# Block 0's q on GpSimd's DMA queue, in a fused attention and feed-forward kernel with a written-out order

## The chip, the cores and the metric

The kernel runs on one core of a Trainium2 chip. The metric is the time of one execution on the device in microseconds (us). A core has five engines with instruction queues of their own: TensorE (PE, matmuls; its weight loads are listed apart as PEld), VectorE (DVE), ScalarE (ACT), GpSimd (POOL) and SyncE (SP, which here only issues DMAs). Each works through its queue in order and waits on semaphores for the others. SP, ACT and POOL can issue DMAs.

## The reference

Chunked causal attention over 4 batches, 8 heads, 768 positions and 64 dimensions, and then a gated feed-forward layer on the 3072 tokens of 512 numbers. From each chunk of 32 keys a minimum and a maximum are formed, from these an upper bound for each query and chunk, and each query looks at the six chunks with the highest bounds:

```python
ub = sum(maximum(q * k_min, q * k_max), axis=-1)      # per query and chunk, causal
top_chunks = argsort(ub)[..., -6:]
scores = where(chosen & causal, q @ k.T / 8, -1e9)
x = softmax(scores) @ v                               # (3072, 512)
xn = x / sqrt(mean(x * x) + 1e-6) * rms_g
out = (silu(xn @ w_gate) * (xn @ w_val)) @ w_out      # d_ff 1536
```

## The kernel before, in words

The work is cut into 12 blocks of 256 tokens (batch b, third m of the sequence), taken in the order of ORDER (L340): the blocks with m = 0 of all four batches first. "Block 0" is (0, 0), "block 1" is (1, 0). Each block has two head groups of four heads (g = 0, 1; operation names end in it). For each block:

- **Loads.** load_qk (L431) brings k and q into the tiles kraw and qraw (128 partitions: four heads x 32 rows). For blocks 0 to 2 (PACKED) each of the two comes in four DMAs, one for each head of a group (a = 0 to 3), with 32 partitions and both head groups in each: 128 KB a DMA. load_v (L456) brings v in two halves, load_w (L464) and load_wo (L469) the feed-forward weights in three thirds each (wg0 to wg2, wv0 to wv2, wo0 to wo2), all of these cast to bf16 on the way and issued by POOL. "load q0020" is q of block (0, 0), head 2.
- **Selection.** DVE turns k and q (turn, L636), reduces k to minima and maxima (ext0, ext1, L651), dk subtracts (L657); bd0 and bd1 place them for PE (L676); PE forms the bounds (upper, L540); DVE turns them back (ubn), bars the future (bar), finds the sixth largest (top), compares (mk) and turns the mask (mt); swap copies it for the other half. half (L643) makes bf16 copies of k and q.
- **Attention.** PE forms the scores (L760, the mask by L771), ACT the exponentials (exp, L810), POOL cuts the triangle (tri, L780), PE multiplies with v (values, L836), DVE divides (rden L851, norm L855). Blocks 0 and 1 do this in two parts (a and b).
- **Feed-forward.** square (ACT, L872), rms (POOL), scale, the turn of x on PE (turn, L916), xsT; then the gate matmuls wg and wv (L960), tanh, tg, vcopy, hh, and project (L1007), out, store. For block 0 the gates go by halves of 128 tokens in pieces of four column tiles: "wg(0, (0,)).4" is block 0, first half, tiles 4 to 7, which need wg1; the pieces .0 need wg0 and wv0, the pieces .4 wg1 and wv1, the pieces .8 wg2 and wv2.

None of this is put in order at run time. The kernel records every operation with its engine (and for some a choice of engines), and the class Plan holds two lists, STEPS and SLOTS (L47, L156): the order in which the recorded operations are issued with the engine of each, and the buffer that each takes. STEPS was found by a search with a planner's costs. Negative numbers in it are fills: matmuls on the identity that keep PE going where the planner saw nothing for it (keep_busy, L1071; narrow ones of 128 columns, wide ones of 512).

Every DMA goes through dma (L370). Its queue is the engine's that issues it. For waiting on them the program has eight semaphores for the DMAs of SP and ACT together and others for POOL's, given out in turn: a DMA first waits for the landing of the one that had its semaphore before. In the program before, the first eight DMAs of SP and ACT are block 0's k (two by each) and q (ACT: heads 0 and 3; SP: heads 1 and 2); then come block 1's eight on SP (k heads 0 and 1, q 0 and 1, k 3, q 2 and 3, k 2). The first load of block 2 also waits for wg1, that of block 3 for wo0 (HELD). POOL issues, behind its first memsets, wv0, v of block 0 (first half), wg1, v of block 0 (second half), v of block 1 (first half), wg0, then relu and the first triangles, v of block 1 (second half), wv1; later wg2, wv2 and the thirds of wo.

Of the kernel before, what the change touches and what calls it, by code (L numbers as in the profile page):

```python
# [11 lines left out]
ACT = mybir.ActivationFunctionType  # L12
# [21 lines left out]
class Plan:  # L34
# [13 lines left out]
        123, 228, 233, 155, 3, 99, 249, 244, 27, 257, 276, 83, 34, 203, 139, 281, 67, 268, 107, 315,  # L48
        131, 75, 115, 291, 380, 396, 323, 412, 538, 428, 466, 299, 404, 473, 482, 420, 443, 490,
        436, 545, 42, 307, 388, 498, 522, 506, 515, 179, 594, 529, 611, -2624, -320, 616, 562, 601,  # L50
        672, 554, 626, 571, 681, 50, 578, 457, 786, 587, 634, -82, -82, 792, 642, 689, 650, 57, 848,
        699, 802, 810, 9, 818, 857, 658, 826, 865, 834, 1098, 665, 875, 841, -176, 704, 451, 1042,
        -112, 736, 912, 713, 1114, 1107, 721, 1058, 1185, -146, 880, 1049, 1066, 19, 731, 1660, 746,
        331, 922, 889, 1130, 1628, 897, 754, 1075, 1644, 930, 1684, -274, -114, 1248, 1170, 961,
        760, 1676, 1082, 1091, 907, 195, 936, 1257, 1362, 1668, -80, 1192, 1138, 971, 1177, 1636,
        1202, 1147, 977, 1210, 770, 1154, 1163, 778, 1123, 1265, 946, -112, 984, 1652, 954, 1368,
        1218, 1001, 994, 1275, 1424, 1226, 1433, -51, 1312, 1378, 8384, 1011, 1234, 1441, 1322,
        1242, 1386, 8344, 1330, 147, 1451, 1017, 1394, 1402, 339, 1280, 1410, 8369, 1418, 1024,
        1289, 347, 1488, 8336, 1498, 1297, 1034, 355, 8401, 1506, 1456, 8353, 1307, 8480, 8410,
        1537, 363, 8362, 1336, 8497, 8488, 1547, 1346, 1762, 1473, 8528, 8506, 1465, 1851, 8513,  # L60
        1354, 1483, 1778, 8536, 8545, 8379, 1553, 1706, 1512, 8561, 8392, 1522, 371, 1530, 1834,
        1560, 1577, 8523, 8432, 1570, 8417, 8554, 1587, 8696, 8449, 1722, 8571, 8688, 8458, 8721,
        1730, 1593, 8584, 8705, 1802, 1739, 171, 2001, 1747, 1600, 8714, 1755, 8576, 8609, 1610,
        1841, 8731, 1856, 8440, 1713, 2212, 1866, 8427, 1794, 2228, 8736, 8593, 1874, 2260, 1811,
        8465, 1771, 2268, 8602, 8784, 2276, 1882, 2244, 1890, 8792, 1818, 1827, 1898, 8475, 8801,
        1906, 8753, 8832, 8817, 1699, 8762, 1912, 2220, 8810, 8849, 8619, 2008, 2308, 1921, 8744,
        2236, 2018, 1691, 1937, 2026, 2252, 2034, 8624, 8769, 2042, 8858, 1931, 1785, 2050, 8779,
        2284, 2057, 2324, 8888, 2292, 2354, 3050, 2064, 2363, 2300, 8632, 1947, 2073, 2316, 2370,
        8656, 2347, 2332, 2378, 2089, 2868, 2426, 2083, 8913, 2804, 8641, 2387, 2820, 2450, 2099,
        1952, 2844, 2442, 8827, -51, 2104, 8664, 2828, 1962, 2410, 8880, 2852, 8673, 2459, 2114,  # L70
        2395, 2900, 1970, 2417, 2403, 1976, 2122, 2836, 8840, 8897, 2482, 2884, 1986, 8928, 8906,
        8865, 2466, 2475, 2499, 3611, 2507, 1994, 8923, 2128, 8945, 2512, 2924, 2138, 2146, 2153,
        2916, 8875, 2161, 2860, 8936, 2522, 3476, 8954, 2171, 8976, 2812, 2530, 2538, 8684, 2946,
        2177, 3508, 2546, 8961, 2186, 2908, 2554, 8971, 2892, 2962, 2561, 2192, 2876, 2986, 9008,
        2433, 3484, 2339, 2201, 3010, 3524, 3532, 2491, 3034, 3540, 3019, 2970, 2568, 3492, 3003,
        3066, 8984, 2577, 9136, 3083, 8994, 2593, 2587, 3026, 9040, 4148, 9153, 3516, 2603, 2656,
        3116, 9162, 9057, 2979, 3043, 9048, 4283, 2953, 3500, 9066, 2665, 9004, 3058, 9096, 3075,
        4212, 9073, 2675, 3108, 9088, 3618, 2681, 163, 9083, 4252, 9121, 3634, 9144, 3092, 9105,
        3642, 2691, 3100, 9240, 9114, 9169, 3588, 2608, 9131, 9016, 9265, 3556, 2618, 2626, 2696,
        4164, 9025, 2632, 2706, 2714, 2720, 9179, 4236, 9184, 2730, 2745, 3572, 2642, 2650, 4220,  # L80
        2738, 3131, 9232, 9201, 3682, 4228, 3123, 2753, 9192, 4180, 9210, 211, 9249, 4244, 3706,
        2763, 3136, 9217, 9258, 2777, 9227, 9280, 3146, 3596, 2769, 5596, 3625, 9275, 9288, 3154,
        3658, 3564, 2993, 3580, 3162, 2784, 3675, 9313, 3548, 9328, 3691, 2793, 4196, 3722, 2931,
        4260, 4172, 9297, 3170, 4204, 9400, 9306, 4268, 4860, 3178, 9496, 9323, 9425, 9036, 3738,
        3185, 4156, 9392, 3698, 3651, 4188, 3755, 9336, 4290, 9409, 3603, 3764, 3192, 4330, 9521,
        3780, 9488, 3747, 9418, 3201, 3772, 3715, 4402, 9435, 9345, 9440, 4306, 3217, 9360, 3730,
        4347, 4417, 3788, 4339, 9457, 4354, 4876, 9505, 3667, 9466, 8652, 3211, 3232, 4378, 4452,
        2939, 9514, 4884, 9536, 3241, 5532, 4314, 3227, 4444, 9448, 3803, 9553, 4428, 3249, 3795,
        9562, 9544, 4868, 4370, 9473, 3304, 1620, 9569, 4386, 4322, 3808, 4436, 4394, 3313, 9579,
        4916, 3329, 9592, 4908, 3818, 9483, 4892, 4297, 9368, 4924, 3826, 9617, 3834, 3344, 3323,  # L90
        4940, 9377, 4980, 3339, 3256, 3353, 4972, 3842, 3280, 4900, 9584, 4459, 3290, 3361, 4932,
        3266, 3850, 9531, 9632, 3274, 9601, 3298, 3857, 3368, 9610, 5548, 3392, 3378, 9649, 4956,
        9627, 9640, 3386, 3402, 4964, 3417, 3410, 3864, 5580, 9658, 4275, 3425, 5644, 9680, 5002,
        3873, 9356, 4363, 5106, 4948, 3889, 3435, 5564, 5066, 9665, 9388, 3458, 3904, 4465, 5628,
        3442, 9675, 5612, 9712, 3913, 5018, 3883, 3452, 5026, 3899, 3921, 5090, 3468, 5042, 3976,
        5082, 4472, 5059, 3985, 5604, 5122, 5035, 4411, 4001, 9688, 4482, 3995, 9720, 9697, 5139,
        4016, 4490, 4498, 5049, 4011, 5148, 3928, 9729, 6308, 3952, 4025, 3938, 6356, 5098, 9792,
        3962, 4506, 5172, 4033, 9840, 3970, 5156, 3946, 9809, 4514, 5164, 4040, 9865, 9800, 9818,
        5620, 4521, 6332, 4050, 5714, 9832, 5572, 5114, 5588, 4592, 9849, 5179, 5652, 4058, 4064,
        5636, 5187, 4601, 9826, 9928, 6316, 5011, 4074, 9858, 4089, 5540, 187, 5075, 9880, 4082,  # L100
        6244, 4609, 5723, 6340, 5192, 6364, 4097, 6292, 9953, 4528, 4107, 5202, 9897, 9920, 4537,
        9906, 6324, 4114, 9752, 9937, 5556, 4130, 4547, 4553, 4124, 9968, 5730, 9777, 9946, 4563,
        4568, 9985, 4140, 5786, 9875, 5129, 9976, 5674, 4577, 91, 6260, 9994, 9888, 5803, 4585,
        6426, 4995, 5812, 9744, 9914, 6284, 4616, 10002, 6276, 9761, 5738, 4640, 9740, 5820, 4626,
        9770, 4664, 6268, 6442, 10072, 4673, 5690, 6348, 6980, 4634, 10256, 4689, 4683, 5210, 7628,
        5218, 5747, 10089, 7020, 10080, 10281, 219, 9963, 4650, 4704, 10098, 4658, 4987, 10120,
        6300, 4713, 6252, 5226, 10208, 7036, 10105, 5754, 5795, 5828, 10137, 10160, 4721, 9787,
        10146, 10168, 6506, 5698, 4728, 6521, 5234, 10177, 5707, 6540, 10008, 5683, 10193, 5762,
        7644, 10115, 5241, 6386, 7028, 10186, 5836, 10225, 4737, 6402, 6548, 10248, 10203, 6450,
        7676, 10128, 4745, 10234, 6988, 6371, 9708, 6410, 10016, 5771, 6916, 10296, 6490, 4699,  # L110
        10025, 7636, 10265, 5248, 6532, 10154, 10313, 4776, 6556, 10274, 5257, 6466, 6996, 4752,
        5273, 5267, 6948, 6474, 10304, 5843, 6956, 4762, 4770, 10036, 5667, 5288, 10322, 4786,
        10216, 5778, 5851, 5297, 7755, 7652, 4794, 10040, 4801, 7660, 10330, 6419, 4809, 5283, 7004,
        10242, 7012, 5305, 6483, 6435, 6498, 4819, 5856, 6457, 10291, 5360, 5866, 7692, 10048, 7724,
        5369, 4826, 5312, 6932, 5336, 5385, 6940, 5379, 10336, 6964, 5346, 5322, 10057, 5874, 5395,
        5330, 7684, 6569, 5882, 5659, 4836, 5400, 6562, 4842, 6576, 5409, 5354, 4852, 5890, 10368,
        5417, 5898, 7732, 6586, 6513, 7098, 5906, 10344, 7115, 6924, 5424, 7708, 10354, 5448, 7740,
        5912, 5434, 5458, 10068, 7058, 10376, 7748, 5921, 5442, 7067, 10496, 6594, 10364, 6602,
# [987 lines left out]
```

## Time and profile before

| | |
|---|---|
| median of 3 runs | 294.74 us (293.15 to 296.25) |
| the profiled execution's own time | 293.79 us |
| its span in the profile | 292.1 us |
| PE busy | 279.0 us, 4718 matmuls |
| DVE, ACT, POOL busy | 215.7, 207.1, 167.8 us |
| DMA | 31.94 MB moved, mean 109 GB/s |
| granted TensorE clock | full in all 40 slices |

The span is shorter than the execution's time by what lies around it. "Busy" counts instructions that compute; a PE that is busy may be doing fills. A line of a group reads: source line, engine, operation, what it writes <- what it reads, count, then the busy time and the mean of one. In a timeline a row begins with its start and duration in us from the span's start, and ends with the number of instructions merged and, in brackets, how long the engine stood idle before it and what ended that. In the chain of waits a row is start, duration and what the chain went through. A row of the DMA issues has the size of one and the median time from issue to landing; for a single DMA that is its own. A row of waits has the total, the count and the longest. A row of windows has, for PE, PEld, DVE, ACT and POOL in turn, the busy time in that stretch and the number of instructions.

### The profile page before, as it was taken

The page shows a single profiled execution, that of the slowest core. Times are in us where ns is not written, and L with a number is a line of the kernel's source. Part 1 is how long each engine was busy: PE and PEld are TensorE (multiplying, and loading weights), DVE is VectorE, ACT ScalarE, POOL GpSimd, SP SyncE. Part 2 cuts the span into 40 slices and gives each one's busy share as a digit, 9 for nine tenths or more (in the row PEclk, how much of TensorE's full clock was granted, in tenths as well). Part 3 has the DMA queues.
Part 4 walks back from the last instruction along what each step waited for, and adds up shares of the span by engine and source line. Part 5 has one row for each costly group of instructions (what it writes and reads, how often), then busy time and mean ns, then how long its engine had stood idle before and what let it go on. Part 6 is the DMA issues. An engine that isn't in the chain of part 4 may idle for free.

```text
span 292.1 us, 11448 instructions
## 1 busy us (share of the span) xinstructions
PE 279.0 (96%) x4718; PEld 214.8 (74%) x4746; DVE 215.7 (74%) x626; ACT 207.1 (71%) x355; POOL 167.8 (57%) x268
## 2 busy tenths in 40 slices
PE   7979999999999899999999999999999999999994
PEld 7637887668877757888676786688678967688663
DVE  3778887889898799799989999987564715374240
ACT  2958887678888898877876595877679766564421
POOL 9649789879888785567683385427125116113410
PEclk9999999999999999999999999999999999999999
DMA  7999999988589584459599816912012300311022
GB/s 177 210 193 224 204 207 134 168 132 127 115 159 159 133 161 87 106 102 168 99 187 139 147 31 92 122 11 74 0 43 69 21 2 3 110 45 30 2 108 72
DMA packets 86388, 31.94 MB, mean 109 GB/s; under 512 B 74816, under 2 KB 81728, under 8 KB 86336
## 3 DMA queue, kind: packets, MB, share of 16 engines
q1 hardware_dynamic: 55776, 22.82, 33.9%
q0 software_dynamic: 29712, 7.87, 27.1%
q10 hardware_dynamic: 848, 0.53, 0.9%
q8 instruction: 37, 0.61, 0.9%
q14 instruction: 15, 0.12, 0.1%
HBM read 28.58 MB, written 6.29 MB: 119 GB/s over the span
## 4 chain that ended last, share of the span: by engine, by line
PE 84%; DMA 7%; DVE 5%; issue 2%; ACT 1%; DVEq 0%; SPq 0%
PE F L960 43%; PE F L1007 19%; PE S L760 7%; PE F L836 7%; DMA kraw<-in_k_dram 6%; PE S L771 3%; PE F L522 3%; DMA xsT<-xs 1%; PE F L540 1%; DVE kx L651 1%; DVE kT L636 1%; DVE xnat L855 1%; PE F L916 1%; DVE xs L890 1%; DVE tg L971 0%
## 5 line engine op out<-in xcount | busy, mean ns | idle before, releaser
L810 ACT ACTIVATE pt<-S 128x1024 bf16<-128x1024 f32 (+3 forms) x104 | 85.5, 858 | 29.7 <-PE S L771 26.4
L982 POOL TENSOR_TENSOR hh<-tg,vs 128x512 bf16<-128x512 bf16 x48 | 55.5, 1165 | 46.4 <-DVE tg L971 29.1
L960 PE MATMUL F<-xsT,wg 128*128 128x256 bf16 (+1 forms) x640 | 72.4, 262 | 0.2 <-DMA xsT<-xs 0.2
L960 PE MATMUL F<-xsT,wv 128*128 128x256 bf16 (+1 forms) x640 | 71.8, 262 | 0.6 <-issue 0.5
L1007 PE MATMUL F<-wo,hh 128*128 128x512 bf16 (+1 forms) x272 | 65.7, 370 | 2.3 <-issue 0.6
L971 DVE SCALAR_TENSOR_TENSOR tg<-th,F 128x512 bf16<-128x512 bf16 x72 | 48.3, 678 | 25.9 <-ACT th L967 19.6
L960 PEld LDWEIGHTS <-wg 128*128 128x128 bf16 x640 | 55.9, 98 | 9.2 <-issue 0.9
L960 PEld LDWEIGHTS <-wv 128*128 128x128 bf16 x640 | 56.2, 98 | 8.5 <-issue 1.0
L967 ACT ACTIVATE th<-F 128x512 bf16<-128x512 f32 x72 | 42.5, 599 | 13.9 <-PE F L960 12.6
L780 POOL TENSOR_SCALAR_AFFINE_SELECT pt<-pt 128x512 bf16<-128x512 bf16 x48 | 31.6, 665 | 27.9 <-ACT pt L810 27.7
L1007 PEld LDWEIGHTS <-hh 128*128 128x128 bf16 x300 | 27.5, 98 | 25.8 <-issue 1.0
L979 ACT ACTIVATE vs<-F 128x512 bf16<-128x512 f32 x48 | 28.5, 599 | 9.8 <-PE F L960 6.5
L760 PE MATMUL S<-qb,kb 32*128 32x256 bf16 (+1 forms) x800 | 32.8, 253 | 0.3
L651 DVE TENSOR_REDUCE kx<-kT 128x16 f32<-128x512 f32 x48 | 31.1, 669 | 0.2
L836 PE MATMUL F<-VX,pt 128*128 128x65 bf16 x672 | 27.5, 194 | 2.9 <-DMA VX<-in_v_dram 1.7
L836 PEld LDWEIGHTS <-pt 128*128 128x128 bf16 x672 | 25.4, 98 | 6.5 <-issue 3.3
L975 DVE TENSOR_TENSOR hh<-tg,F 128x512 bf16<-128x512 bf16 x24 | 16.1, 681 | 10.3 <-PE F L960 10.0
L760 PEld LDWEIGHTS <-kb 32*128 32x128 bf16 x800 | 13.6, 92 | 13.1 <-issue 11.6
L376 POOL DMA_DIRECT2D VX<-in_v_dram x24 | 22.7, 947 | 0.0
L771 PE MATMUL S<-mtd,chunkrow 32*128 32x128 bf16 (+2 forms) x384 | 20.3, 203 | 0.7 <-DVE xnat L855 0.7
L855 DVE TENSOR_TENSOR xnat<-F,rden 128x256 bf16<-128x256 f32 x48 | 19.5, 415 | 0.7
L771 PE MATMUL S<-mto,chunkrow 32*128 32x128 bf16 (+2 forms) x384 | 19.9, 203 | 0.0
(73 smaller groups left out, 337.3 us busy)
## 6 DMA issues: line engine op xcount, KB each, us to landing
out_dram<-osb SPq DMA_DIRECT2D x23, 256.0 KB, 3.0
kraw<-in_k_dram SPq DMA_DIRECT2D x72, 64.0 KB, 3.3
qraw<-in_q_dram SPq DMA_DIRECT2D x72, 64.0 KB, 3.1
VX<-in_v_dram POOLq DMA_DIRECT2D x24, 128.0 KB, 5.1
QX<-qT SPq DMA_DIRECT2D x32, 64.0 KB, 2.4
wv<-in_moe_w_val_dram POOLq DMA_DIRECT2D x3, 512.0 KB, 8.5
wg<-in_moe_w_gate_dram POOLq DMA_DIRECT2D x3, 512.0 KB, 13.5
wo<-in_moe_w_out_dram POOLq DMA_DIRECT2D x3, 512.0 KB, 10.2
```

The lines of the kernel that those rows point to most:

```text
L651: plan.op(f"ext{n}{J}", "DVE", 0.585, 0.67, lambda n=n, op=op: VE.tensor_reduce(out=at(kx)[:, g, n], in_=at(kT).rearrange("p h (j c x) -> ...
L760: TE.matmul(s[a // 2][:, a % 2, c0:c0 + q1 - q0], kbt[r, t, ks], qbt[r, t, q0:q1], start=(t == 0), stop=(t == 1 and not mask), skip_group_ ...
L771: TE.matmul(o, chunkrow[r, BLK * kg + P * e:BLK * kg + P * (e + 1)], mv, start=False, stop=(d == 1), skip_group_check=True)
L780: GE.affine_select(out=d, in_=d, compare_op=ALU.is_ge, fill=0.0, base=0, pattern=[[0, 4], [1, P]], channel_multiplier=-1)
L810: lambda pt=pt, hs=hs, c0=c0, c1=c1, x=sc[hp]: SE.activation(out=at(pt)[:, hs, c0:c1], in_=at(x)[:, :, c0:c1], func=ACT.Exp, scale=SCALE), ...
L836: TE.matmul(o[:, a, :], p_[:, a, off:off + P], vt[:, e, 4 * g + a, :], start=(kb_ == 0 and a == 0), stop=(kb_ == nkb - 1 and a == 3), skip ...
L960: TE.matmul(at(p_)[:, n * W:(n + 1) * W], w[:, g, ht * P:(ht + 1) * P], at(xT)[:, g, x0:x0 + W], start=(g == 0), stop=(g == NP - 1), skip_ ...
L967: plan.op(f"tanh{U}.{hp}", "ACT", 0.48, 0.6, lambda th=th, gp=gp: SE.activation(out=at(th), in_=at(gp), func=ACT.Tanh, scale=0.5), pri - 0 ...
L971: VE.scalar_tensor_tensor(out=at(tg), in0=at(th), scalar=1.0, in1=at(gp), op0=ALU.add, op1=ALU.mult), pri - 30, reads=[th, gp], writes=[tg ...
L979: plan.op(f"vcopy{U}.{hp}", "ACT", 0.48, 0.6, lambda vs=vs, vp=vp: SE.activation(out=at(vs), in_=at(vp), func=ACT.Copy), pri + 0.1, reads= ...
L982: plan.op(f"hh{U}.{hp}", "POOL", 1.11, 1.16, lambda tg=tg, vs=vs, hh=hh: GE.tensor_tensor(out=at(hh), in0=at(tg), in1=at(vs), op=ALU.mult) ...
L1007: TE.matmul(at(op)[:, cs], at(key)[:, o:o + P], wo[:, ht, cs], start=(ht == 0), stop=(ht == NHT - 1), skip_group_check=True)
```

## The change

load_qk gets two sets. A tensor in WHOLE is loaded in two DMAs, one for each head group g, each over all 128 partitions (256 KB), and not in four DMAs of 32 partitions; one in BYPOOL is issued by POOL. Both sets hold block 0's q alone. So four DMAs of SP and ACT become two of POOL. The recorded operations are fewer by two, and STEPS and SLOTS are new throughout.

```diff
+    WHOLE = {(0, 'q')}
+    BYPOOL = {(0, 'q')}
...
     def load_qk(i, nm, src):
         b, m = ORDER[i]
         key = (nm + "raw", b, m)
-        first = True
-        for a in (0, 2, 1, 3):
...
+        todo = []
+        if (i, nm) in WHOLE:
+            for g in range(NG):
+                sv = src[b].rearrange("(g a) (m r j) d -> g m a r (j d)", g=NG, m=NBLK, r=32)[g, m]
+                todo.append((f"g{g}", sv, lambda g=g: at(key)[:, g].rearrange("p j h d -> p (j h d)"), 8, 0.09, (g,)))
+        else:
+            for a in (0, 2, 1, 3):
...
+        first = True
+        engs = ("POOL",) if (i, nm) in BYPOOL else ("SP", "ACT") if i == 0 else ("SP",)
+        for x, sv, dst, packets, cost, gs in todo:
+            dma(f"load {nm}{b}{m}{x}", engs, sv, dst, packets, cost,
+                loads_due(i, nm == "q"), writes=[key + (g,) for g in gs],
...
```

In the new program the first eight DMAs of SP and ACT are block 0's k and then, on SP, block 1's q head 0 and k heads 0, 3 and 1; the other four of block 1 (q 2 and 1, k 2, q 3) follow, each behind the landing of one of block 0's k loads or of block 1's first q load. POOL issues, behind two memsets, the identity's steps and two more memsets, q of block 0 (group 0), a memset, q (group 1), v of block 0 (first half), wg1, v (second half), wv0, and after the first small steps of the selection v of block 1 (first half), wg0, its second half, wv1; later wg2, wv2 and the thirds of wo. dk of block 0's first group moves from DVE to POOL. The load of ACT's table moves from behind block 0's first exponentials to ACT's start.

DVE's order in the first blocks, where it differs most: pat stands before and own behind the first turns of k; block 1's k is turned (group 1) ahead of block 0's top of group 1, and (group 0) ahead of its mk and mt; then come one reduction of block 1, rden of block 0, the turn of block 1's q, rden, another reduction, and the two norms. Before, block 0's mt came first, then the turns of block 1's q and k, two reductions, the two rden, a third reduction and the two norms.

PE's order up to the first gate holds the same operations. Of fills there are 87 narrow and 24 wide (before 92 and 34); one of two wide ones now stands ahead of wg(0, (0,)).8, and the one between values of block 2 is gone. After the first gates, one values operation of block 1 and the turn of its first half come ahead of the first use of wv1, in which the two halves' .4 pieces now follow each other.

More of the change, by code (lines that the diff above doesn't have):

```diff
@@ L433, in load_qk @@
         key = (nm + "raw", b, m)
-        first = True
-        for a in (0, 2, 1, 3):
-            rows = slice(32 * a, 32 * (a + 1))
-            if i in PACKED:
-                sv = src[b].rearrange("(g a) (m r j) d -> a m r g (j d)", a=4, m=NBLK, r=32)[a, m]
-                todo = [(sv, lambda rows=rows: at(key)[rows].rearrange("r g j h d -> r g (j h d)"), 4, 0.12, (0, 1))]
-            else:
-                todo = []
+        todo = []
[5 more added lines that the diff above has]
+            for a in (0, 2, 1, 3):
+                rows = slice(32 * a, 32 * (a + 1))
+                if i in PACKED:
+                    sv = src[b].rearrange("(g a) (m r j) d -> a m r g (j d)", a=4, m=NBLK, r=32)[a, m]
+                    todo.append((f"{a}0", sv, lambda rows=rows: at(key)[rows].rearrange("r g j h d -> r g (j h d)"),
+                                 4, 0.12, (0, 1)))
+                    continue
@@ L442, in load_qk @@
                 for g in range(NG):
                     sv = src[b, 4 * g + a, BLK * m:BLK * (m + 1), :].rearrange("(j r) d -> r j d", r=32)
-                    todo.append((sv, lambda rows=rows, g=g: at(key)[rows, g].rearrange(
+                    todo.append((f"{a}{g}", sv, lambda rows=rows, g=g: at(key)[rows, g].rearrange(
                         "r j h d -> r j (h d)"), 16, 0.019, (g,)))
-            for k_, (sv, dst, packets, cost, gs) in enumerate(todo):
-                dma(f"load {nm}{b}{m}{a}{k_}", ("SP", "ACT") if i == 0 else ("SP",), sv, dst, packets, cost,
-                    loads_due(i, nm == "q"), writes=[key + (g,) for g in gs],
-                    takes=[(key, nm + "raw")] if first else (), reads=() if first else [key],
-                    behind=[HELD[i]] if i in HELD and first else ())
-                first = False
+        first = True
@@ L453, in loads_due @@
+        engs = ("POOL",) if (i, nm) in BYPOOL else ("SP", "ACT") if i == 0 else ("SP",)
+        for x, sv, dst, packets, cost, gs in todo:
+            dma(f"load {nm}{b}{m}{x}", engs, sv, dst, packets, cost,
+                loads_due(i, nm == "q"), writes=[key + (g,) for g in gs],
+                takes=[(key, nm + "raw")] if first else (), reads=() if first else [key],
+                behind=[HELD[i]] if i in HELD and first else ())
+            first = False
     def loads_due(i, n):
```

278 rows, old and new, of tables (SLOTS, STEPS) are left out of this document.

## The prediction

> **What bounds the kernel now.** I read the page first, then the chain of waits from 0 to 40 us, the waits of PE, the timeline of each engine over the first 40 us, and the landing times of single DMAs.
>
> ```profile
> span 292.1 us, 11448 instructions
> PE 279.0 (96%) x4718; PEld 214.8 (74%) x4746; DVE 215.7 (74%) x626; ACT 207.1 (71%) x355; POOL 167.8 (57%) x268
> DMA  7999999988589584459599816912012300311022
> ```
>
> PE is busy for 96% of the span, and the third row shows the transfers full from slice 2 to slice 8 (a slice is 7.3 us), that is until about 58 us. So the kernel is bound by PE's own work, except where PE has nothing real to do yet: at the start. There the chain that sets the end runs through a load of block 1's k, and from it through DVE, ACT and PE to the first feed-forward matmuls:
>
> ```profile
> 9.67 7.49 DMA kraw<-in_k_dram
> ...
> 25.43 1.79 PE F L960 x32
> ```
>
> That load is issued only at 9.67 because of the program's eight DMA semaphores for SP and ACT together: block 0's k and q take all eight, and each later load waits for the landing of the one eight places earlier; this one waits for block 1's first load. It lands at 17.16. DVE turns it, and only behind that stand, in DVE's order, block 0's rden and norm (to 21.09), then on the other engines square, rms, scale, the turn of x, and the first gate at 25.27. From there on PE runs almost without a break, as its waits and its timeline show:
>
> ```profile
> PE F L836 <- DMA VX<-in_v_dram: 1.7, 1, 1.7
> PE F L836 <- issue: 1.0, 1, 1.0
> PE S L771 <- DVE xnat L855: 0.7, 1, 0.7
> ```
> ```profile
> 25.27 1.05 PE L960 MATMUL F<-xsT,wg 128*128 128x128 bf16 x16
> ...
> 33.15 1.06 PE L960 MATMUL F<-xsT,wv 128*128 128x128 bf16 x16
> 34.05 0.42 PE L836 MATMUL F<-VX,pt 128*128 128x65 bf16 x8
> 34.31 1.05 PE L960 MATMUL F<-xsT,wv 128*128 128x128 bf16 x16
> 35.20 0.39 PE L916 MATMUL F<-ident,xs 128*128 128x128 bf16 x4
> 35.42 1.24 PE L960 MATMUL F<-xsT,wg 128*128 128x128 bf16 x16
> ```
>
> Only the wait of 1.7 us for v lies ahead of the first gate; the one of 0.7 lies between the first two rows of the timeline. So whatever brings the stream of gate matmuls forward by x us, and keeps it fed, shortens the span by x.
>
> **The change part by part.**
>
> *The loads of block 1.* Block 0's q leaves SP and ACT (four DMAs), so the eight semaphores hold block 0's k and four loads of block 1 at once. The last load of block 1's k then waits for one of block 0's k loads, the first DMAs of the program, and is issued near 4.5 (an estimate: block 0's k is whole at 5.09, when DVE turns it) instead of 9.67. With the 7.49 us of the chain's row it lands at 12.0, which I take, since all eight loads are in flight together. The ends are 9.6 (with the 5.1 us of the row for q below) and no gain at all, 17.16.
>
> *DVE's new order.* DVE now turns block 1's k before it finishes block 0's second head group. First the busy time of two stretches (DVE is the third group of three), then rows of DVE's timeline:
>
> ```profile
> 5.09:13.40 8.31, 8.18 (x158) 6.29 (x160) 7.90 (x28) 6.52 (x12) 5.74 (x12) 1.00 1.33 212
> 17.24:21.09 3.85, 3.85 (x65) 1.84 (x63) 3.85 (x10) 2.28 (x4) 3.42 (x8) 1.00 1.70 188
> ```
> ```profile
> 1.97 0.29 DVE L398 TENSOR_REDUCE own<-ident 128x2 f32<-128x128 bf16 x1 [1.97 <-POOL ident masks.py:199]
> ...
> 7.74 0.17 DVE L657 TENSOR_TENSOR kx<-kx 128x16 f32<-128x16 f32 x1
> 8.07 0.71 DVE L636 STREAM_TRANSPOSE qT<-qraw 128x512 f32<-128x512 f32 x1 [0.16 <-DMA qraw<-in_q_dram]
> ...
> 12.63 0.24 DVE L581 MAX8 m<-ubn 128x8 f32<-128x8 f32 x2
> 12.78 0.23 DVE L591 STREAM_TRANSPOSE mtd<-mk 128x64 bf16<-128x64 bf16 x1
> 12.93 0.19 DVE L587 TENSOR_TENSOR mk<-ubn,m 128x64 bf16<-128x64 f32 x1
> 13.16 0.24 DVE L591 STREAM_TRANSPOSE mtd<-mk 128x64 bf16<-128x64 bf16 x1
> 16.27 0.71 DVE L636 STREAM_TRANSPOSE qT<-qraw 128x512 f32<-128x512 f32 x1 [2.87 <-DMA qraw<-in_q_dram]
> ```
>
> From 5.09 to 13.40 DVE does block 0's work almost without a gap (7.90 of 8.31), then it stands still until 16.27. In the new order this stretch loses dk (0.17, to POOL) and passes top, mk and mt of the second group (0.24, 0.19, 0.24) behind the first turn of block 1's k; own and pat, two small reductions of like size, change places around the first turn. So DVE asks for block 1's k at 13.40 - 0.17 - 0.67 = 12.6, and the k of 12.0 is there: no wait. From that turn to the end of norm stand the second stretch (3.85, all of it DVE work), the 0.67, and a turn of q (0.71, the row at 16.27), less about 0.4 for a third reduction that falls behind: 4.8. Norm ends at 17.4 instead of 21.09, 3.7 sooner. From there to the first gate the operations are the same (25.27 - 21.09 = 4.2), so **the chain would allow the first gate at 21.6, 3.7 us sooner**.
>
> *q by GpSimd's queue.* POOL's first DMA of before, wv0, was issued at 2.79; the two for q stand behind fewer memsets, the first near 2.3, which is an estimate. DVE wants q at 8.0 (the row at 8.07). How long can it take? Landing times:
>
> ```profile
> qraw<-in_q_dram SPq DMA_DIRECT2D x2, 128.0 KB, 5.1
> ```
> ```profile
> 2.79 0.97 POOL L376 DMA_DIRECT2D wv<-in_moe_w_val_dram  x1
> ```
> ```profile
> wv<-in_moe_w_val_dram POOLq DMA_DIRECT2D x1, 512.0 KB, 8.3
> ```
> ```profile
> VX<-in_v_dram POOLq DMA_DIRECT2D x1, 128.0 KB, 12.0
> ```
>
> SP's q took 5.1 us. On POOL's queue wv0, which stood first, took 8.3 for 512 KB; v took 12.0, but stood behind wv0. A q DMA has 256 KB and stands first, so it is nearest to SP's row: 5.3 for the first (there at 7.6, no cost), one us more for the second (8.6, wanted near 10). Ends: 5.1 (no cost), and v's 12.0 (there at 14.3, 6.3 late). v's first half still passes ahead of the 512 KB that it stood behind, so the 1.7 us wait goes; it lay beside the wait for k and is worth nothing by itself. All weights move behind q.
>
> [...]
>
> *The weights, which the new order wants sooner.* Here the gain is cut. Issues on POOL, and landings:
>
> ```profile
> 18.71 0.78 POOL L376 DMA_DIRECT2D wv<-in_moe_w_val_dram  x1
> ...
> 26.41 0.84 POOL L376 DMA_DIRECT2D wg<-in_moe_w_gate_dram  x1
> 27.24 0.75 POOL L376 DMA_DIRECT2D wv<-in_moe_w_val_dram  x1
> ```
> ```profile
> wv<-in_moe_w_val_dram POOLq DMA_DIRECT2D x1, 512.0 KB, 11.8
> ```
> ```profile
> wg<-in_moe_w_gate_dram POOLq DMA_DIRECT2D x1, 512.0 KB, 6.6
> wv<-in_moe_w_val_dram POOLq DMA_DIRECT2D x1, 512.0 KB, 8.5
> ```
>
> wv1 landed at 18.71 + 11.8 = 30.5 and was first used at 33.15; wg2 landed at 33.0 and was used at 35.42: 2.6 and 2.4 us to spare. The transfers were full all the while, and the set that must pass until wg2 is there (blocks 0 to 2, four halves of v, five thirds of weights) is the same in the new order. So I leave these landings where they are. Before, 7.9 us lay between the first gate and wv1's first use, 0.7 of them the wait; in the new order one pair of values (0.26, 34.05 to 34.31) and one turn (0.22, 35.20 to 35.42) stand ahead of it too: 7.7, so it is wanted at 29.3 and waits until 30.5. Two gate groups (0.89 each, 34.31 to 35.20) and a fill later comes wg2's use, at 32.7, and wg2 is there at 33.0 instead of 35.42. **So 2.4 us are gained, and 1.3 of the chain's 3.7 are given back to wv1 and wg2.** wv2 landed at 27.24 + 8.5 = 35.7 and is wanted about three gate groups after wg2: no wait.
>
> *The rest.* The fills of PE stand where PE waits anyway; ten wide ones fewer count nothing, and had they no such cover they would be 10 x 0.23 = 2.3 us, by this row:
>
> ```profile
> 18.05 2.55 PE L1074 MATMUL F<-ident 128*128 128x512 bf16 x11
> ```
>
> One fill that stood late, in the full stream, goes: 0.2. The later orders are new on all engines, but the work is the same, and PE has no wait above 1.0 us after the first gate, so there is little to win; I take 0, between -0.8 and +1.5. Sum: -2.4 - 0.2 = -2.6. The profiled execution took 293.79 us (span 292.1), the median of the three runs is 294.74, 0.95 more: 291.2 against the first, **292.1 against the median**, which I predict.
>
> **The rivals.**
>
> *No gain: transfers, not issues, are the limit.* The eight loads of block 1 share the same DMA engines with q, v and weights; issued sooner they only queue longer. For it: the full DMA row. Against: weights that shared the time before 17.16 were not wanted until 25, so k can take their place. Landing at L, k costs nothing up to 12.6 + 1.2 = 13.8 (the wait for wv1 hides that much) and the gain is gone at 16.2. L near 16 gives 294. [...]
>
> *Slower: a late load holds DVE.* The turn of block 1's k stands ahead of block 0's top, mk, rden and norm on DVE, which is in order. If k still lands at 17.16, norm ends at 17.2 + 4.8 = 22.0, 0.9 later than before: 295.6. If q lands as late as v did, 6.3 us, less the 1.2 that wv1 hides: -2.6 + 5.1, 297.2. It decides from a q later than 8.0 + 1.2 + 2.6 = 11.8. Against: q is first on its queue.
>
> *Weights keep up.* POOL issues wv1 and wg2 sooner too; if the transfers finish 1.3 us sooner by that, or because q goes in two DMAs instead of four, the chain's 3.7 stand: 294.74 - 3.9 = 290.8.
>
> **How the numbers follow.** Forecast (a gain of 1.5 to 3.4): 0.47. Weights keep up (over 3.4): 0.20. No gain (1.5 to 0): 0.18. Slower: 0.15. The range goes from the fast case with 0.8 more from the later orders, 290.0, to k at 17.16, 295.6; beyond lie a q as late as v and late losses. About 1% (2.9 us) is what a measurement of this kernel can tell from no change. Below 291.8 lie the fast case and a quarter of the forecast: 0.32 faster by over 1%. Above 297.7 lies only a late q together with losses later: 0.07. Within 1%: 0.61.
>
> **What would show it.** Right: the last load of block 1's k issued before 6 and landed before 13.8; DVE's turn of it near 12.6; norm of block 0 ending near 17.4; the first gate near 21.6; then PE waiting 1 to 1.5 us in all for wv and wg before 33; wg2's first use near 33.0. Wrong: DVE idle for q beyond 9, or for k beyond 14; wv1 and wg2 landing elsewhere than at 30.5 and 33.0; or PE waits of over 1 us after 60 us.

## The result, and the profile after

The changed kernel takes 298.89 us (median of 4 runs, 297.72 to 300.01) against 294.75 us (4 runs): the ratio is 1.0142, with a 95% interval from 1.0099 to 1.0186. It is slower by 1.4%, where 292.1 us was predicted, with a range from 290.0 to 295.6. The profiled execution took 299.3 us. Medians in this document are over all runs of a kernel, ratios over the undisturbed ones.

The page of the changed kernel, the rows that answer to those of before (a slice is 7.4 us):

```profile
span 297.5 us, 11437 instructions
PE 280.3 (94%) x4704; PEld 215.8 (73%) x4731; DVE 217.7 (73%) x627; ACT 209.4 (70%) x359; POOL 165.6 (56%) x265
PE   7398799989999989999999999999999999999994
PEclk9959999999999999999999999999999999999999
```

The span is 5.4 us longer, and PE does 1.3 us more work in it. What differs most is in the second and third slice: PE is busy 3 tenths of the second, and in the third its clock was granted at half, which did not occur before. The chain of waits says why:

```profile
2.10 10.77 DMA qraw<-in_q_dram
...
12.89 0.72 DVE qT L645
...
13.64 1.09 ACT qb L652
...
14.77 0.40 PE S L769 x7
```

The chain now starts with q and not with block 1's k. PE's first wait is for its bf16 copy, and DVE, on its timeline, waits 5.30 us for q; the two q loads take 10.8 and 12.2 us from issue to landing:

```profile
PE S L769 <- ACT qb L652: 5.1, 1, 5.1
```
```profile
12.89 0.71 DVE L645 STREAM_TRANSPOSE qT<-qraw 128x512 f32<-128x512 f32 x1 [5.30 <-DMA qraw<-in_q_dram]
15.23 0.71 DVE L645 STREAM_TRANSPOSE qT<-qraw 128x512 f32<-128x512 f32 x1 [0.16 <-DMA qraw<-in_q_dram]
19.20 0.71 DVE L645 STREAM_TRANSPOSE kT<-kraw 128x512 f32<-128x512 f32 x1
```
```profile
qraw<-in_q_dram POOLq DMA_DIRECT2D x1, 256.0 KB, 10.8
```
```profile
qraw<-in_q_dram POOLq DMA_DIRECT2D x1, 256.0 KB, 12.2
```
```profile
29.63 1.05 PE L969 MATMUL F<-xsT,wv 128*128 128x128 bf16 x16
```

q was turned at 8.07 before and is turned at 12.89 now, 4.8 later. Block 1's k is turned at 19.20, and no transfer is named for it: DVE comes to it late, the data lay there. The first gate (last row) comes at 29.63 instead of 25.27, 4.4 later. From the first gate to the end of the span it is 297.5 - 29.63 = 267.9 us, before 292.1 - 25.27 = 266.8. So the loss was made ahead of the first gate and carried to the end nearly one for one, with 1.0 us on top.

### The profile page after: what moved, and what is told of

Read it like the earlier page. It is cut to its first block, busy times and chain, and to the rows that moved or that the text cites. A ratio compares the mean times of both kernels' runs of the same rounds, so it can differ in the third digit from the quotient of the medians.

```text
span 297.5 us, 11437 instructions
## 1 busy us (share of the span) xinstructions
PE 280.3 (94%) x4704; PEld 215.8 (73%) x4731; DVE 217.7 (73%) x627; ACT 209.4 (70%) x359; POOL 165.6 (56%) x265
## 4 chain that ended last, share of the span: by engine, by line
PE 78%; DVE 8%; DMA 5%; issue 3%; SPq 2%; ACT 2%; POOL 1%; DVEq 0%; ACTq 0%; POOLq 0%
PE F L969 39%; PE F L1016 19%; PE S L769 6%; PE F L845 6%; DMA qraw<-in_q_dram 5%; PE S L780 2%; PE F L531 2%; SPq L378 2%; PE F L549 2%; DVE kx L660 2%; DVE qT L645 1%; DVE xnat L864 1%; PE F L925 1%; DVE tg L980 1%; PE F L1083 1%
## 5 line engine op out<-in xcount | busy, mean ns | idle before, releaser
L991 POOL TENSOR_TENSOR hh<-tg,vs 128x512 bf16<-128x512 bf16 x48 | 56.1, 1174 | 38.2 <-DVE tg L980 21.5
L980 DVE SCALAR_TENSOR_TENSOR tg<-th,F 128x512 bf16<-128x512 bf16 x72 | 48.2, 678 | 17.0 <-ACT th L976 12.6
L789 POOL TENSOR_SCALAR_AFFINE_SELECT pt<-pt 128x512 bf16<-128x512 bf16 x48 | 30.8, 647 | 36.8 <-ACT pt L819 36.5
L769 PEld LDWEIGHTS <-kb 32*128 32x128 bf16 x800 | 13.9, 93 | 18.9 <-issue 17.1
L645 DVE STREAM_TRANSPOSE qT<-qraw 128x512 f32<-128x512 f32 x24 | 16.6, 694 | 7.0 <-DMA qraw<-in_q_dram 6.4
L780 PEld LDWEIGHTS <-chunkrow 32*128 32x128 bf16 x768 | 18.7, 94 | 2.5 <-issue 1.7
## 6 DMA issues: line engine op xcount, KB each, us to landing
wv<-in_moe_w_val_dram POOLq DMA_DIRECT2D x3, 512.0 KB, 12.6
```

What stands on the lines that cost most here:

```text
L769: TE.matmul(s[a // 2][:, a % 2, c0:c0 + q1 - q0], kbt[r, t, ks], qbt[r, t, q0:q1], start=(t == 0), stop=(t == 1 and not mask), skip_group_ ...
L780: TE.matmul(o, chunkrow[r, BLK * kg + P * e:BLK * kg + P * (e + 1)], mv, start=False, stop=(d == 1), skip_group_check=True)
L789: GE.affine_select(out=d, in_=d, compare_op=ALU.is_ge, fill=0.0, base=0, pattern=[[0, 4], [1, P]], channel_multiplier=-1)
L980: VE.scalar_tensor_tensor(out=at(tg), in0=at(th), scalar=1.0, in1=at(gp), op0=ALU.add, op1=ALU.mult), pri - 30, reads=[th, gp], writes=[tg ...
L991: plan.op(f"hh{U}.{hp}", "POOL", 1.11, 1.16, lambda tg=tg, vs=vs, hh=hh: GE.tensor_tensor(out=at(hh), in0=at(tg), in1=at(vs), op=ALU.mult) ...
```

## The experiments

The q loads of the change read [4 heads][32 rows][512 numbers] from memory into 128 partitions; the loads they replace read [32 rows][2 head groups][512]. Four theories of the loss:

- **F, few engines.** With 4 heads outermost, only 4 of the 16 DMA engines carry all 256 KB of a q load. This was the author's conjecture, which e5 tests (a DMA share of 0.26 with 4 outermost, of 1.02 with 128). The prediction did not weigh it.
- **Q, queue.** GpSimd's queue is slow in itself.
- **C, contention.** Block 1's loads, issued sooner, take q's share of the engines.
- **K, clock.** The half clock after PE's wait costs time of its own.

All medians of whole kernels, with the three events that the reasoning uses, from DVE's and PE's timelines of the profiled run of each (q and k: the start of the first turn of block 0's q and of block 1's k; gate: the first gate matmul). Each ratio is to runs of the kernel before made beside that kernel; their medians are 294.21 to 294.88:

| kernel | median us (runs) | ratio to before, interval | q | k | gate |
|---|---|---|---|---|---|
| before | 294.75 (4) | 1 | 8.07 | 17.24 | 25.27 |
| after | 298.89 (4) | 1.0142 [1.0099, 1.0186] | 12.89 | 19.20 | 29.63 |
| e1 four loads on POOL | 297.8 (10) | 1.0081 [1.0039, 1.0122] | 10.44 | 16.75 | 28.31 |
| e2 two loads on ACT | 301.25 (4) | 1.0219 [1.0155, 1.0283] | 11.43 | 20.49 | 30.92 |
| e3 four loads on SP, ACT | 295.52 (10) | 1.0011 [0.9976, 1.0046] | 7.78 | 14.19 | 24.31 |
| e4 after, 80 fills more | 299.34 (4) | 1.0163 [1.0095, 1.023] | 11.40 | 16.65 | 26.77 |
| e6 q rows in one piece | 294.09 (10) | 0.9993 [0.9952, 1.0033] | 8.50 | 13.80 | 24.23 |
| e7 block 1 held | 302.75 (4) | 1.0234 [1.0151, 1.0317] | 8.87 | 21.33 | 33.73 |
| e8 before, q alone moved | 298.85 (4) | 1.0147 [1.0091, 1.0203] | 12.37 | 20.67 | 32.03 |
| e9 e3, 40 fills more | 296.16 (10) | 1.0048 [1.002, 1.0075] | 8.61 | 15.61 | 26.62 |
| e10 e3, 80 fills more | 296.74 (10) | 1.0079 [1.0043, 1.0114] | 7.69 | 16.54 | 26.86 |
| e11 before, k first | 294.05 (12) | 0.997 [0.9936, 1.0003] | 7.84 | 13.10 | 24.69 |
| e12 e11, rmsg later | 293.42 (12) | 0.9978 [0.9945, 1.001] | 7.99 | 13.27 | 24.34 |

**e1: four loads of 32 partitions, still on POOL.** In the order, each of the two loads became two.

```diff
-    WHOLE = {(0, 'q')}
+    WHOLE = set()
```

> The changed kernel with block 0's q still on GpSimd's queue, but in four DMAs of 32 partitions and both head groups (as all other loads of blocks 0 to 2), in the places of the two; nothing else moves. Theory F (few engines: the source of a DMA of 128 partitions has the four heads as its outermost dimension, and so only 4 of the 16 DMA engines carry its 256 KB): the four DMAs use all engines, q is whole by 9 to 10 us instead of 12.9 and 15.2, the first gate comes near 25 instead of 29.8, 294 us. Theory Q (GpSimd's queue gets too small a share beside SP's, whatever the shape): q is whole no sooner than 13, about 299. Theory C (block 1's eight loads, issued sooner, take the engines from q): also no sooner than 13, about 299.

The chain's row for the last of the four, and DVE's wait:

```profile
3.96 6.35 DMA qraw<-in_q_dram
```
```profile
10.44 0.71 DVE L653 STREAM_TRANSPOSE qT<-qraw 128x512 f32<-128x512 f32 x1 [2.93 <-DMA qraw<-in_q_dram]
```

The last of the four, 128 KB each, lands at 3.96 + 6.35 = 10.3; in the change the last of the same 512 KB landed at 3.04 + 12.2 = 15.2, on the same queue. That is against Q. But q is turned at 10.44 and not by 10, the gate comes at 28.31 and not near 25, and the time missed the 294 that F gave: it lies nearer to the 299 of Q and C. One part is that every one of these loads carries both head groups: the first turn needs all four, and POOL issues the last only at 3.96. Another part is PE's clock, which is taken up behind e10.

**e2: the two loads of 128 partitions, on ACT's queue.** They stand behind k's loads there.

```diff
-    BYPOOL = {(0, 'q')}
+    BYPOOL = set()
```

> The changed kernel with block 0's q in the same two DMAs of 128 partitions, but issued by ACT behind its two loads of k, 0.4 us sooner than GpSimd did. They take two of the eight semaphores, so two more of block 1's loads wait. F: the shape is the cause, q is still late, the first group at 10 or later, and the kernel is above 296 us. Q: off GpSimd's queue q is there by 8, and the kernel gives the forecast 292. C: somewhat fewer loads compete; q by 9 to 11, 294 to 297.

The chain's row for the second load:

```profile
2.92 14.36 DMA qraw<-in_q_dram
```

Away from POOL the loads are as late (q at 11.43) or later: the second group is turned at 17.31, 5.9 behind the first, where it was 2.3 behind it on POOL. Q is refuted. This is the slowest of the four ways to load q with the new order (after, e1, e2, e3).

**e3: four loads on SP and ACT, as before; the rest of the change stays.** Both edits above.

> The changed kernel with block 0's q in four DMAs of 32 partitions on ACT (heads 0, 3) and SP (heads 1, 2), as in the kernel before; the new orders of all else stay. q takes four of the eight semaphores again, so block 1's k is issued late again, and DVE waits for it. By F and Q alike q is there at 8; block 1's k lands near 16 to 17, and DVE, which now turns it ahead of block 0's second group, stands till then: first gate 25 to 26, 294.5 to 296 us. By C q is there at 8 too, since block 1's loads wait. What it tells: whether the new orders are worth anything without the move of q, and whether the harm lies in them (then it is near 299) or in the move.

DVE turns q at 7.78 without a wait, and the time is that of before: without the move of q, the change is worth nothing and costs nothing. Block 1's k came sooner than I expected: its last load, issued at 7.96, landed 6.1 us later, and DVE turned it at 14.19. Block 1's loads are issued sooner in this kernel too, so C alone does not make q late.

**e4: the changed kernel with 80 narrow fills more** in PE's first fill (one number of the order).

> The changed kernel with 80 more narrow fills on PE behind the first 79, so that PE does not stand idle for 5 us while block 0's q is late. Theory K (the idle PE loses its granted clock, 0.50 from 15 to 20 us, and that costs time of its own): the clock stays at 1.00, the matmuls of the bounds take 0.44 us instead of 0.65, and 1 to 2 us of the 4.1 lost come back: about 297.3. Against it: DVE and ACT set the pace there and nothing comes back, 298.9.

PE's windows of after and of e4, in that order; columns are the stretch, its length, PE's busy time and matmuls, granted clock, DMA share (it adds up the times of the packets, and so can pass 1) and GB/s:

```profile
12.50:15.00 2.50, 0.23 (x8) 0.91 1.51 182
15.00:17.50 2.50, 2.50 (x43) 0.50 1.44 189
...
20.00:22.50 2.50, 2.38 (x44) 0.73 1.46 217
```
```profile
15.00:17.50 2.50, 2.14 (x50) 1.00 1.62 172
...
60.00:90.00 30.00, 27.68 (x391) 0.94 0.73 126
```
```profile
62.70 0.36 PE L556 MATMUL F<-qT,BO 64*64 64x32 f32 x10 [1.91 <-DVE xnat L871]
```

The clock is whole again there and the first gate comes 2.9 us sooner, yet the median does not move. Of the 2.9 us, 1.5 are q's: in this profiled run its first load landed in 9.3 us and it was turned at 11.40, and nothing here shows that the fills did that. Further on in the same run PE catches up with DVE at 60.8, waits 1.91 us for a norm (last row), and the clock falls there instead.

**e5: the loads by themselves.** A kernel of its own: one load at a time, DVE waits for each.

```diff
+    by4 = [q[b].rearrange("(g a) (m r j) d -> g m a r (j d)", g=2, m=3, r=32)[g, m]
+           for b, g, m in ((0, 0, 0), (1, 1, 1), (2, 0, 2), (3, 1, 0))]
+    by128 = [q[b].rearrange("h s d -> (h s d)").rearrange("(x p n) -> x p n", p=128, n=512)[x]
+             for b, x in ((0, 0), (1, 1), (2, 2), (3, 3))]
...
+    for x in by4:
+        nc.gpsimd.dma_start(out=t[:, 0:512], in_=x)
+        seen(0)
...
```

> Nothing of the reference is computed: six kinds of load run one after the other, four times each, with nothing beside them, and zeros are written out. Kinds: 256 KB to 128 partitions from 4 heads x 32 rows (outermost dimension 4, the shape of the change's q) or from 128 rows in one piece (outermost dimension 128), and 256 KB to 32 partitions from 32 rows x 4 heads (outermost dimension 32), each on GpSimd's queue and on SP's. Theory F (the first shape's bytes go to 4 of the 16 DMA engines): 64 KB on each of 4 engines instead of 16 KB on each of 16; with 410 GB/s as the most that a slice of the trace after shows, so 25.6 GB/s for one engine, that is 2.5 us against 0.6: the first shape lands about 1.9 us later than the second, on both queues alike. Theory Q (GpSimd's queue is what is slow): no difference by shape, GpSimd's loads over 2 us longer than SP's. Theory C (only contention in the kernel): all six within 0.7 us of each other.

The rows of each line's summary: first POOL with by4, with by128, then SP with by4 (DVE's wait for the four), then SP with by128.

```profile
DMA to landing us min/median/max: 5.4/5.5/5.7
```
```profile
DMA to landing us min/median/max: 2.7/2.7/2.9
```
```profile
  DVE s L22: 21.9, 4
```
```profile
  DVE s L22: 10.9, 4
DMA to landing us min/median/max: 2.5/2.6/2.7
```

256 KB to the same partitions land in 5.5 us with 4 outermost and in 2.7 with 128 outermost. SP shows the same pair as waits, 21.9 / 4 = 5.5 and 10.9 / 4 = 2.7. With 32 outermost POOL's took 3.2; two of these four loads read the very rows that loads with 4 outermost read, so it is not where the rows lie in memory. The shape makes the difference and the queue almost none, with nothing beside it. DMA's share differs as well. Two windows on SP's queue, one in a load with 4 outermost, one in a load with 128 (the last three columns are the clock, DMA's share of the 16 engines and GB/s):

```profile
42.00:42.20 0.20, 0.00 (x0) 0.00 (x0) 1.00 0.26 102
62.80:63.00 0.20, 0.00 (x0) 0.00 (x0) 1.00 1.02 399
```

With 4 outermost the share stays at 0.26 and the rate at 102 GB/s from 41.6 to 43.2, a quarter of what the other shape reaches. 0.26 of 16 is 4.2: it is what 4 engines of 16 would show, at 25.5 GB/s each, as F had it, though the profile does not name the engines. The 2.8 us between the shapes is more than the 1.9 that F gave (by F, 48 KB more on an engine in 2.8 us is 17 KB per us on average), since the transfer with 4 outermost starts slowly: 45, 25 and 53 GB/s in the three half microseconds from 40.0.

**e6: the changed kernel, q's loads with 128 rows outermost.** It reads 128 other rows and leaves out those that block 0 needs; queue, place in the order, size and destination are those of the change.

```diff
-                sv = src[b].rearrange("(g a) (m r j) d -> g m a r (j d)", g=NG, m=NBLK, r=32)[g, m]
+                sv = src[b].rearrange("h s d -> (h s d)").rearrange("(x p n) -> x p n", p=P, n=512)[g]
```

> The changed kernel, but GpSimd's two loads of block 0's q read 128 consecutive rows instead of 4 heads x 32 rows: same queue, same issue times, same 256 KB to the same 128 partitions, other data (so block 0's q of batch 0 is another one and the output isn't the reference's). Theory F: all 16 engines carry it; DVE turns the first head group at 7.6 to 9 (12.89 in the trace after) and the second without a wait, TensorE's wait for qb falls from 5.1 to under 2 us, the first gate comes at 24.3 to 26.5 (29.63), and the time is 295 to 296.5. Theories Q and C: nothing changes, q is turned at 12 to 13 and the time is 298 to 300.

```profile
qraw<-in_q_dram POOLq DMA_DIRECT2D x1, 256.0 KB, 6.4
```
```profile
qraw<-in_q_dram POOLq DMA_DIRECT2D x1, 256.0 KB, 6.9
```
```profile
8.50 0.71 DVE L645 STREAM_TRANSPOSE qT<-qraw 128x512 f32<-128x512 f32 x1 [0.99 <-DMA qraw<-in_q_dram]
10.61 0.70 DVE L645 STREAM_TRANSPOSE qT<-qraw 128x512 f32<-128x512 f32 x1
13.80 0.71 DVE L645 STREAM_TRANSPOSE kT<-kraw 128x512 f32<-128x512 f32 x1
```

One line takes the landing from 10.8 and 12.2 to 6.4 and 6.9 and the whole loss away; the time is even below the range that F gave. This is the test that decides for F in the kernel.

**e7: block 1's loads held until q has landed.** In the order, three of block 1's loads moved behind q's second.

```diff
-    HELD = {2:("wg",1),3:("wo",0)}
+    HELD = {1:("qraw",0,0,1),2:("wg",1),3:("wo",0)}
```

> The changed kernel, with block 1's eight loads held until block 0's q has landed. Theory C (block 1's loads, issued sooner, take q's bandwidth): q lands as in the kernel before, DVE turns it at 7.6 to 8.5. Theory F (four engines): these four still have 2 x 64 KB of q, 5.1 us at 25.6 GB/s, and their share of k, v and the weights, so q is turned at 9.5 to 11. In both block 1's k is now issued after q and lands some 5 us behind, 14 to 17; the first gate is at 26 to 29, the time 295.5 to 298.5. If q still comes at 12 to 13, neither contention nor the share of four engines is the cause.

```profile
qraw<-in_q_dram POOLq DMA_DIRECT2D x1, 256.0 KB, 6.7
```
```profile
qraw<-in_q_dram POOLq DMA_DIRECT2D x1, 256.0 KB, 7.1
```
```profile
3.04 7.12 DMA qraw<-in_q_dram
...
12.94 8.21 DMA kraw<-in_k_dram
```

With 4 outermost, but without block 1's loads beside it, q lands in 6.7 and 7.1 and is turned at 8.87, between what C and F had. So F does its full harm only together with C: the shape alone costs little here (q at 8.87, against 8.50 in e6), and so do block 1's loads alone (e6). An estimate from e5's average of 17 KB per us: block 1's eight loads are 1 MB; spread evenly they put 64 KB on each engine, 3.7 us more for the four that, by F, carry q; measured are 10.8 - 6.7 = 4.1 and 12.2 - 7.1 = 5.1. The time itself missed my range upwards: the last load of block 1's k is issued only at 12.94 and takes 8.21, so the gate comes at 33.73.

**e8: the kernel before, with q alone moved**, by the two sets of the change, ahead of POOL's other loads.

> The kernel before with only the move of q: GpSimd's two loads of 128 partitions, ahead of its other DMAs, every other instruction in the order of before. Theory F: the four engines are as full as in the changed kernel's opening, since k is loaded ahead of q in both; q is turned at 10 to 13 (8.07 before), the first gate is 2 to 5 us later than 25.27, time 296.5 to 299. Theory N (the new order of the rest is what costs): 293.5 to 295, q by 9.

q is turned at 12.37 and the ratio is 1.0147, that of the whole change; the gate, 6.8 us later, is later than the 2 to 5 that F had. SP's timeline of this kernel:

```profile
0.80 1.81 SPq L385 DMA_DIRECT2D kraw<-in_k_dram  x4
```

Behind block 0's two k loads, two loads of block 1's k go out before 2.61, since q has left the semaphores to them; in the kernel before, block 1's first was issued at 3.87. So C comes with the move and needs no new order.

**e9 and e10: e3 with 40 and 80 narrow fills more.**

> The kernel of e3 (all of the change but q's move: q by four DMAs on SP and ScalarE) with 40 narrow filling matmuls more in TensorE's first fill, some 1.6 us of PE by the 3.4 us that 80 took in e4. Theory K (a wait of 1.3 us of TensorE at 9.7 us costs 3.4 us of half clock, 0.86 and 0.50 in the windows of e3, and this costs time of its own): the clock stays 1.00 through 30 us, the first gate comes 0.5 to 1.2 us sooner than e3's 24.31, and the time is 293.5 to 295 (e3 295.52). Rival (DVE sets the gate, the clock's loss lies beside it): gate 24.0 to 24.6 and time 295 to 296.

> As e9 with 80 fills more. Theory K: clock 1.00, but the fills now run past the arrival of qb and push the first scores back by about 1 us: 294 to 296. Rival (DVE sets the gate): as e9, within 0.5 us of it.

A window of e3, one of e10:

```profile
12.50:15.00 2.50, 2.50 (x49) 0.50 1.64 182
```
```profile
12.50:15.00 2.50, 2.50 (x62) 1.00 1.58 191
```

With 80 fills the clock is full through 250 us, and the kernel is 0.8% slower than before: the first scores come at 13.49 and not at 9.66, and the gate at 26.86. With 40, k's landing also came later (DVE waits 2.19 us for it), and the clock fell later (0.70 from 17.5 to 20). Both are misses for K, and e9's gate, and both times by 0.1 to 0.2 us, lie outside what the rival gave too: buying the clock back with fills brought nothing here.

At the gate the clock does show, though no time here prices it. Against e6 (q 8.50, gate 24.23), q is 1.9 later in e1 and the gate 4.1; in after 4.4 and 5.4; but in e4, where the clock was whole, 2.9 and only 2.5. Against the kernel before, q is 4.3 later in e8 and the gate 6.8. In e1 and e8 the chain from the first scores to the gate runs mostly through PE and its fills, and the granted clock is 0.50 from 12.5 to 20 in e1 and from 15 to 22.5 in e8. Five wide fills, in e8's chain:

```profile
19.16 2.25 PE F L1090 x5
```

In the kernel before, five took 1.25 at full clock. So where PE lost its clock while it waited for q, the gate slipped by 1 to 2.5 us beyond q's own lateness. That is a second cost of the late q and no rival to F; what it is worth in time these runs do not separate.

**e11: the kernel before, block 1's k first.** SP's loads of block 1 in the order k, k, k, k, q, q, q, q, and DVE's first turn of block 1's q (with its bf16 copy) behind the turns of k and one reduction. This is the prediction's first gain by itself.

> The kernel before with one thing of the change, block 1's k issued sooner: SP's loads of block 1 in the order k, k, k, k, q, q, q, q (k's last was the eighth), and DVE turns block 1's k ahead of its first q; nothing else moves. Theory P (the prediction's step on the loads was right and the change spoils it with q): k is turned at 13.5 to 14.5 (17.24 before, after a wait of 2.87 for q), the first gate comes at 21.5 to 23.5 (25.27), and the time is 291 to 293. Rival R (the chain from k to the gate isn't what sets the gate: DVE's other work and block 1's q, which now lands later, take its place): gate at 24 to 25.5, time 293.5 to 295.

DVE's rows and the chain:

```profile
13.10 1.30 DVE L644 STREAM_TRANSPOSE kT<-kraw 128x512 f32<-128x512 f32 x2
16.19 0.71 DVE L644 STREAM_TRANSPOSE qT<-qraw 128x512 f32<-128x512 f32 x1 [1.21 <-DMA qraw<-in_q_dram]
```
```profile
16.97 1.08 POOL qb L652
...
18.09 0.58 POOL pt L788
...
20.64 0.30 PE F L844 x4
...
23.30 0.77 PE F L548 x30
...
24.74 1.90 PE F L968 x32
```

k is turned 4.1 us sooner (13.10), and the gate comes 0.6 sooner. The chain has gone over to block 1's q, from there to POOL, which copies q and only then cuts the triangle that block 0's values wait for, and then to PE's own work. Theory R holds. The time is lower than before by 0.3%, with an interval that just includes none.

**e12: as e11, and rmsg's load issued later**, so that the last q load gets a semaphore sooner.

> As e11, and ScalarE issues rmsg's load behind block 0's exponentials, so that block 1's last q load no longer waits for block 1's first k load to land (9.04 us in e11) but for one of block 0's q loads. Theory L (that wait is what holds q, and q now holds the gate): the last q load is issued by 7.5, q is turned at 14 to 15 without or with little wait (16.19 in e11 after 1.21), the first gate comes at 22.5 to 24 (24.69), and the time is 292 to 293.5. Rival B (the 16 DMA engines are full in that time, so issuing sooner lands no sooner): q at 15.5 to 16.5, gate at 24 to 25, time 293.5 to 294.5.

q is turned at 15.84 after a wait of 0.70, and the gate comes at 24.34, both as B has them; the chain now runs through the first half of v, and from 14.99 on almost only through PE:

```profile
4.34 10.61 DMA VX<-in_v_dram
...
14.99 0.35 PE F L844 x6
```

The median, 293.42, is the lowest of all and on the border between the two theories; the interval includes no change.

## Why the prediction was wrong

- **"q by GpSimd's queue" is the step that failed and made the loss.** It put q's landing at 5.3 us "nearest to SP's row", by place in the queue and bytes. The term was mis-sized: 10.8 and 12.2 us, the far end of its bounds (12.0). What it compared was unlike: SP's row is a load with 32 outermost. e5 gives 5.5 against 2.7 us for the shape alone and a DMA share of 0.26 against 1.02, e6 shows that with all else as in the change the shape makes the loss, e7 that it needs block 1's loads beside it, e8 that the move alone is enough for both. Its issue time, 2.3 estimated, was nearly right (2.10). GpSimd's queue itself was not slow: two loads of the good shape landed on it in 6.4 and 6.9 (e6).
- **The slower rival had the mechanism right and its price too low:** it decides from a q later than 11.8 (12.89). That its 297.2 lies near 298.89 is luck, since it is for a q 6.3 late. q was 4.8 late, and for that the rival's own sum gives -2.6 + 4.8 - 1.2 = 1.0 us more than before, 295.7; measured are 4.1 more. The missing 3 us are mostly the gain of 2.6 in its sum, which was not there even with q in time (e6: 294.09, ratio 0.9993). I set it at too little chance, since the argument "first on its queue" left out the shape of the load (5.5 against 2.7 us in e5).
- **Block 1's loads** went as far as the issue: block 1's last k load at 4.95 (4.5 estimated), landing 10.0 us later at 14.95 and not at 12.0, and covered, since DVE asked only at 19.20. The no-gain rival's contention is real: k took 10.0 us and not 7.49, which was covered, and q's 10.8 us fall to 6.7 without block 1's loads (e7).
- **"From norm to the first gate the same 4.2 us" failed as well.** With q in time (e6) DVE turned block 1's k at 13.80 (12.6 predicted) without a wait for it and ended norm at 18.50, 4.7 us behind it (4.8 predicted); but the gate came at 24.23 and not at 21.6, 5.7 behind norm. The prediction took the operations from norm to gate to be the same. On POOL they are not: before, rms of block 0 stands ahead of dk of block 1's second group, in the new order behind it and behind a triangle and bd1. That dk waits for a reduction that DVE does behind norm. POOL's rows of before, then of e6 (dk writes kx, rms writes ri_all):

```profile
21.93 0.19 POOL L878 TENSOR_TENSOR ri_all<-ss_all,eps 128x1 f32<-128x1 f32 x1 [0.89 <-ACT junk L872]
22.76 0.21 POOL L657 TENSOR_TENSOR kx<-kx 128x16 f32<-128x16 f32 x1
```
```profile
20.18 0.23 POOL L666 TENSOR_TENSOR kx<-kx 128x16 f32<-128x16 f32 x1 [0.72 <-DVE kx L660]
21.17 0.19 POOL L887 TENSOR_TENSOR ri_all<-ss_all,eps 128x1 f32<-128x1 f32 x1
```

Rms starts 2.7 us behind norm in e6 and 0.8 before; the chain of e6, and that of after, runs through these steps. No run has the new order with rms ahead of dk, so what that would bring is not shown. e11 shows that the order of before has little to give as well: k 4.1 sooner, gate 0.6 sooner. Behind the chain that the trace showed lay two others, through block 1's q with POOL's triangle (e11's chain) and through v and PE's fixed order (e12's), which leave 0.6 and 0.9 us. So the gain of 2.4 was not there even with a good load of q.
- **Weights:** they did not stay at 30.5 and 33.0. With q late POOL issued them later, and wv1 landed at 20.92 + 12.6 = 33.5, wg2 at 27.36 + 8.4 = 35.8; in e6 at 15.55 + 13.9 = 29.5 and 21.99 + 10.1 = 32.1. In after the gate was so late that PE waited for neither.
- **Fills and later orders:** the later orders cost 1.0 us from the first gate to the end in after, within the bounds of -0.8 to +1.5. In e6, with the gate 1.0 sooner, it is 292.5 - 24.23 = 268.3, 1.4 more than before, which is where the small gain of that kernel goes. One wait that stands there, for block 1's mask, remains without a named releaser:

```profile
30.01 0.20 PE L780 MATMUL S<-mtd,chunkrow 32*128 32x32 bf16 x4 [1.65 <-issue]
```

- **That the span follows the first gate** was right: from the gate to the end of the span lie 266.5 to 269.9 us in twelve of the thirteen whole kernels, and 265.2 in e8.

## What to carry to other kernels

Before a DMA is priced by its bytes and its place in the queue, look at the outermost dimension of its source: 4 outermost took 5.5 us where 128 took 2.7 with nothing beside, and 10.8 to 12.2 where 6.4 to 6.9 with other loads beside. When a chain of waits is to be shortened, find the second longest first: taking 4.1 us out of this one moved its end by 0.6. And a load taken off a queue let the loads behind it start sooner (two of block 1's k before 2.61, where the first had gone at 3.87: e8), against the very one that was moved (10.8 us to land with block 1's loads beside it, 6.7 without: after and e7).

## What the runs showed of the hardware

The second of two loads with 4 outermost came 5.9 us behind the first on ACT's queue (e2) and 2.3 behind it on GpSimd's (after). Why the two differ is not shown, since the profile does not name the engines that carry a load; it shows their share, 0.26 with 4 outermost against 1.02 with 128 (e5).

The half clock came in pieces near one length. In after the windows from 12.5 to 22.5 us lost 0.09 + 0.50 + 0.50 + 0.27 of 2.5 us each, 3.4 us in all, which at half clock is 6.8 us; in e3 (0.86, 0.50 and 0.96 in the windows from 10 to 17.5) the same working gives 3.4, in e9 (0.70 and 0.62 from 17.5 to 22.5) 3.4, and in e1 (0.82, three of 0.50 and 0.63 from 10 to 22.5) 10.3: once, twice or three times 3.4. Why one wait of 1.3 us lost the clock (e3) and another of 1.7 us (before, ahead of the first gate) did not, no run here shows.
